# RetNet retention feeding a top-1 mixture of experts: retention output transposed, router logits by chunk

## The chip, the cores and the metric

One Trainium2 chip, one core of it. The metric is the device time of one execution in microseconds (us). The profile comes from one execution whose own time stands beside its span below.

## What is computed

For 4 batches, 8 heads, 768 positions and a head width of 64, a state is decayed and added to at each position; the result becomes 3072 tokens of 512 features. Each token goes to the one expert of eight that its logits choose.

```python
gamma = 1.0 - 2.0 ** (-5.0 - np.arange(H, dtype=np.float32))
for t in range(S):
    state = gamma[None, :, None, None] * state + np.einsum('bhd,bhe->bhde', k[:, :, t], v[:, :, t])
    y[:, :, t] = scale * np.einsum('bhd,bhde->bhe', q[:, :, t], state)
...
logits = x @ w_gate
expert_idx = np.argmax(logits, axis=1)
...
h = np.maximum(x_sorted[lo:hi] @ w1[e], 0.0)
y_sorted[lo:hi] = h @ w2[e]
...
return (gate_w[:, None] * y).astype(np.float32)
```

## The kernel before

All products are float32 but the small ones of the routing. The work has three parts.

**Retention.** The sequence is cut into six chunks of 128 positions, and a step is one chunk of one batch (`steps`, 24 of them, the four batches of a chunk in a row). `load` fetches q, k and v four steps ahead, in rows of 256 bytes, on SP's queue. `scale_and_transpose(n)` scales q by the decay of the position (`qs`, DVE) and v by its inverse (`vs`, POOL), and turns q and k heads first (`tr`, eight transposes). `retain(n)` makes the scores of the eight heads (`sc`, two row halves of the array side by side), masks them from PSUM (`am`, DVE), makes the chunk's addition to the state (`new`, two column halves side by side), adds and decays it (`total`, `state`), copies it into a block-diagonal tile (`stb`, POOL), and makes `y`: for each pair of heads one 128x128 product with `stb` and two with the masked scores as the stationary operand and 64 columns of `vs` moving.

**Routing.** `logits(n)`, one step behind, turns the step's `x` (`trx`, four transposes), copies it (`xT`, DVE) and makes `lg` with x stationary and the eight columns of `wg` moving. After the fourth batch of a chunk `place(c)` takes the maximum, the rank of each token within its expert (`rk`) and its slot (`found`), scales x by the gate and writes it to `x_d`. After chunk 4 the first 256 tokens of expert 0 are gathered early (`xs2[0]`).

**Experts.** The early half of expert 0 runs first on PE (`hp<-xTa`, `ye<-hTa`), with the last routing spread between its blocks through the generator `rest`. Then the eight experts follow, each with `layer1`, the transposes of the next one (`turn`) and `layer2`.

Outside the parts under `manual_schedule` a list scheduler orders each engine's instructions; each engine then runs its queue in that order.

## Time and profile before

| | |
|---|---|
| median of 3 runs | 602.84 us |
| lowest, highest | 590.13 us, 608.62 us |
| the profiled execution | 591.75 us |
| its span, mean granted TensorE clock | 589.9 us, 0.954 |

The span runs from the first to the last instruction, and the execution's own time is 1.85 us more. The retention ends near 200 us of the span, the early half of expert 0 near 235 us, and the rest belongs to the experts. A matmul in float32 leaves two records in the trace, a transpose or a bfloat16 product one. A busy PE says little, since the ends of matmuls are modelled; the time from one group's start to the next one's is what a group costs.

### The profile page before, as it was taken

The page shows a single profiled execution, that of the slowest core. Times are in us where ns is not written, and L with a number is a line of the kernel's source. Part 1 is how long each engine was busy: PE and PEld are TensorE (multiplying, and loading weights), DVE is VectorE, ACT ScalarE, POOL GpSimd, SP SyncE. Part 2 cuts the span into 40 slices and gives each one's busy share as a digit, 9 for nine tenths or more (in the row PEclk, how much of TensorE's full clock was granted, in tenths as well). Part 3 has the DMA queues.
Part 4 walks back from the last instruction along what each step waited for, and adds up shares of the span by engine and source line. Part 5 has one row for each costly group of instructions (what it writes and reads, how often), then busy time and mean ns, then how long its engine had stood idle before and what let it go on. Part 6 is the DMA issues. An engine that isn't in the chain of part 4 may idle for free.

```text
span 589.9 us, 7874 instructions
## 1 busy us (share of the span) xinstructions
PE 558.0 (95%) x3160; PEld 374.7 (64%) x3160; DVE 109.6 (19%) x291; ACT 123.3 (21%) x245; POOL 119.0 (20%) x156
## 2 busy tenths in 40 slices
PE   4998999999999998999999999999999999999990
PEld 3988988989898873855545545546545645545540
DVE  2545455534645230300000000000000000000000
ACT  2213222312424130212102202201211301202100
POOL 8322313213221023040032013005005005002010
PEclk9987979959999899899999999999999999999996
DMA  9964745965512122880333325217306217001010
GB/s 185 207 131 122 146 125 130 352 171 115 149 35 73 36 87 89 312 311 20 144 111 148 144 57 191 75 72 258 141 7 242 76 71 257 1 4 53 4 39 21
DMA packets 96469, 72.43 MB, mean 123 GB/s; under 512 B 77946, under 2 KB 77946, under 8 KB 96384
## 3 DMA queue, kind: packets, MB, share of 16 engines
q1 hardware_dynamic: 88096, 52.46, 32.9%
q0 software_dynamic: 5120, 12.60, 5.7%
q10 hardware_dynamic: 3168, 6.29, 2.9%
q8 instruction: 47, 0.77, 0.6%
q14 instruction: 38, 0.31, 0.2%
HBM read 60.84 MB, written 14.68 MB: 128 GB/s over the span
## 4 chain that ended last, share of the span: by engine, by line
PE 54%; issue 34%; DVE 4%; POOL 3%; DMA 2%; SPq 0%; POOLq 0%; DVEq 0%
PE hp L189 13%; PE ye L201 11%; PE y L290 7%; PE sc L262 5%; PE tr L248 4%; PE y L286 4%; PE lg L310 4%; PE new L271 2%; PE trx L305 2%; POOL xs L151 2%; DMA out_dram<-o,dst 1%; PE trs L181 1%; POOL out_dram L208 1%; DVE am L264 1%; DMA q<-in_q_dram 1%
## 5 line engine op out<-in xcount | busy, mean ns | idle before, releaser
L201 PE MATMUL ye<-w2t,hT 128*128 128x512 f32 (+3 forms) x640 | 164.1, 455 | 0.0
L189 PE MATMUL hp<-xTs,w1t 128*128 128x416 f32 (+4 forms) x512 | 163.7, 482 | 0.2 <-DVE xTs L182 0.2
L189 PEld LDWEIGHTS hp<-xTs,w1t 128*128 128x128 f32 x512 | 94.2, 195 | 70.1 <-issue 54.9
L201 PEld LDWEIGHTS ye<-w2t,hT 128*128 128x128 f32 (+3 forms) x640 | 74.8, 154 | 84.4 <-issue 83.2
L208 POOL DMA_INDIRECT out_dram<-o,dst x30 | 29.8, 994 | 281.8 <-ACT o L204 276.0
L290 PE MATMUL y<-vs,am 128*128 128x64 f32 x384 | 60.5, 279 | 1.4 <-DVE am L264 0.7
L290 PEld LDWEIGHTS y<-vs,am 128*128 128x128 f32 x384 | 55.5, 205 | 4.3 <-issue 1.8
L191 ACT ACTIVATE hT<-hp 128x416 f32<-128x416 f32 (+4 forms) x64 | 29.3, 481 | 137.4 <-PE hp L189 94.0
L204 ACT COPY o<-ye 128x512 f32<-128x512 f32 (+3 forms) x40 | 17.7, 444 | 144.8 <-PE ye L201 144.5
L264 DVE TENSOR_TENSOR am<-sc,causal 128x512 f32<-128x512 f32 x48 | 31.3, 685 | 44.8 <-PE sc L262 44.8
L286 PE MATMUL y<-stb,qT 128*128 128x128 f32 x160 | 38.3, 324 | 0.0
L262 PE MATMUL sc<-qT,kT 64*128 64x128 f32 x384 | 37.2, 306 | 0.9 <-DVE am L264 0.9
L151 POOL DMA_INDIRECT xs<-x_d,src x30 | 30.4, 1013 | 33.8 <-DVE dst L174 24.9
L281 POOL COPY stb<-state 64x256 f32<-64x256 f32 x40 | 19.7, 492 | 83.7 <-DVE state L278 72.1
L243 POOL TENSOR_TENSOR vs<-v,dec 128x512 f32<-128x512 f32 x24 | 25.5, 1064 | 40.3 <-PE new L271 26.7
L262 PEld LDWEIGHTS sc<-qT,kT 64*128 64x128 f32 x384 | 29.8, 202 | 5.3 <-issue 4.4
L293 ACT COPY xg<-y 128x512 f32<-128x512 f32 x24 | 14.1, 588 | 86.8 <-PE y L290 86.8
L286 PEld LDWEIGHTS y<-stb,qT 128*128 128x128 f32 x160 | 26.4, 207 | 1.3
L248 PE MATMUL tr<-ident,qs 128*128 128x128 f32 x96 | 19.2, 325 | 7.1 <-DVE qs L242 7.1
L310 PE MATMUL lg<-wg,xT 128*128 128x8 f32 x192 | 25.2, 258 | 0.2
L310 PEld LDWEIGHTS lg<-wg,xT 128*128 128x128 f32 x192 | 24.3, 198 | 1.5 <-DVE xT L307 0.9
L250 ACT COPY qT<-tr 128x512 f32<-128x512 f32 x24 | 14.1, 587 | 39.4 <-PE tr L248 39.4
(111 smaller groups left out, 350.2 us busy)
## 6 DMA issues: line engine op xcount, KB each, us to landing
w1t<-in_moe_w_dram SPq DMA_DIRECT2D x8, 2048.0 KB, 7.9
w2t<-in_moe_w_dram SPq DMA_DIRECT2D x8, 2048.0 KB, 15.0
q<-in_q_dram SPq DMA_DIRECT2D x24, 256.0 KB, 4.3
k<-in_k_dram SPq DMA_DIRECT2D x24, 256.0 KB, 3.3
v<-in_v_dram SPq DMA_DIRECT2D x24, 256.0 KB, 5.1
x_d<-xg ACTq DMA_DIRECT2D x6, 1024.0 KB, 4.3
xs<-x_d,src POOLq DMA_INDIRECT x30
out_dram<-o,dst POOLq DMA_INDIRECT x30
```

Source lines behind the costliest of these rows:

```text
L151: nc.gpsimd.indirect_dma_start(out=xs[:, t, :], out_offset=None, in_=x_d[0:rows, :], in_offset=bass.IndirectOffsetOnAxis(ap=idx[:, t : t + ...
L189: nc.tensor.matmul(hp, lhsT=w1t[:, 0, dt, ts(f, P)], rhs=xT[:, dt, 0:n], start=(dt == 0), stop=(dt == DT - 1))
L191: nc.scalar.activation(out=hT[:, f, 0:n], in_=hp, func=AF.Relu)
L201: nc.tensor.matmul(y[j * m : j * m + m, 0:c], lhsT=hT[:, f, t * P : t * P + m], rhs=w2t[:, 0, f, ts(j, c)], start=(f == 0), stop=(f == FT ...
L208: done = nc.gpsimd.indirect_dma_start(out=out[:, :], out_offset=bass.IndirectOffsetOnAxis(ap=idx[:, t : t + 1], axis=0), in_=o[:, t, :], i ...
L243: nc.gpsimd.tensor_tensor(out=vs, in0=vt, in1=inner(gk, D), op=ALU.mult)
L248: nc.tensor.transpose(tr[:, a, :], src[:, 2 * a : 2 * a + 2, :].rearrange("p h d -> p (h d)"), ident)
L262: nc.tensor.matmul(sc[j][:, a, :], lhsT=kT[r, a, :], rhs=qT[r, a, :], start=True, stop=True)
L264: nc.vector.tensor_tensor(out=am[j], in0=sc[j], in1=middle(causal[:, :], HP), op=ALU.mult)
L286: nc.tensor.matmul(y[:, ts(a, P)], lhsT=qT[:, a, :], rhs=stb[b][c % 2][:, a, :], start=True, stop=False, skip_group_check=True)
L290: nc.tensor.matmul(y[:, ts(h, D)], lhsT=am[j][:, a, :], rhs=vs[:, h, :], start=(c == 0), stop=True, skip_group_check=True)
L310: nc.tensor.matmul(lg[:, b, :], lhsT=xT[:, dt, :], rhs=wg[:, dt, :], start=(dt == 0), stop=(dt == DT - 1))
```

## The change

- q is turned raw, and the scaling is done while it leaves PSUM (`qT`, DVE), by a table `gqT` that keeps the decay of the position in the whole sequence. v is scaled by the inverse of the same decay (one table for each chunk), so the state is only added to: the product with `gp`, the tile `total` and the block-diagonal copies on POOL go. POOL makes one `gqT` for each chunk.
- `y` comes out transposed, features first: for each head one product with the 64x64 state stationary and qT moving, and one with 64 columns of `vs` stationary and the masked scores moving. A pair of heads uses two diagonal quarters of the array (state) and two column halves (scores). ACT copies it into `xTg`, which holds a chunk's four batches.
- The logits are made once for a chunk: four products of 32 columns (`wg`, padded with zeros) with 512 tokens moving, each in a column group of its own (`parts`), a copy on ACT (`lgT`), and four products with the 0/1 matrix `sel` that adds the groups and turns the result (`lg`).
- `place` is a generator for every chunk, advanced twice a step (three times in the last chunk). It turns x back (`trx`, sixteen transposes at its end), and ACT scales x while it leaves PSUM.
- Loads run five steps ahead with six buffers, and expert 0's weights are issued at step 17 in place of 12.

```diff
+    back = [gamma ** -(e + P * c) for c in range(NC)]
+    return np.concatenate([gamma ** e / math.sqrt(D)] + back + [whole], 1).astype(np.float32)
...
+    dec = const.tile([P, (1 + NC) * H + HP], F32, tag="dec", name="dec")
+    wg = const.tile([P, DT, P // DT], F32, tag="wg", name="wg")
+    sel = const.tile([P, E], F32, tag="sel", name="sel")
...
+    gq, gp = dec[:, 0:H], dec[:, (1 + NC) * H :]
+    nc.gpsimd.memset(wg, 0.0)
+    nc.gpsimd.tensor_copy(sel, ident[:, 0:E])
+    for dt in range(1, DT):
+        nc.gpsimd.tensor_tensor(out=sel, in0=sel, in1=ident[:, dt * (P // DT) : dt * (P // DT) + E], op=ALU.add)
...
-        stb = [[keep.tile([P, HP, P], F32, tag=f"stb{b}_{i}", name=f"stb{b}_{i}") for i in range(2)]
-               for b in range(B)]
         xg = [keep.tile([P, B, DM], F32, tag=f"xg{i}", name=f"xg{i}") for i in range(2)]
+        xTg = [keep.tile([P, DT, B, P], F32, tag=f"xTg{i}", name=f"xTg{i}") for i in range(2)]
+        gqT = [keep.tile([P, HP, P], F32, tag=f"gqT{i}", name=f"gqT{i}") for i in range(2)]
...
-                t = att.tile([P, H, D], F32, tag=nm, name=nm, bufs=5)
+                t = att.tile([P, H, D], F32, tag=nm, name=nm, bufs=6)
                 nc.sync.dma_start(t, src[b, :, ts(c, P), :].rearrange("h t d -> t h d"))
                 got.append(t)
             qkv[n] = got
+        def heads_first(src):
+            tr = ps("tr", 3, "tr").rearrange("p (a t) -> p a t", a=HP)
+            for a in range(HP):
+                nc.tensor.transpose(tr[:, a, :], src[:, 2 * a : 2 * a + 2, :].rearrange("p h d -> p (h d)"), ident)
+            return tr
         def scale_and_transpose(n):
+            c, b = steps[n]
             qt, kt, vt = qkv.pop(n)
...
             vs = att.tile([P, H, D], F32, tag="vs", name="vs", bufs=3)
-            nc.vector.tensor_tensor(out=qs, in0=qt, in1=inner(gq, D), op=ALU.mult)
-            nc.gpsimd.tensor_tensor(out=vs, in0=vt, in1=inner(gk, D), op=ALU.mult)
...
+            nc.gpsimd.tensor_tensor(out=vs, in0=vt, in1=inner(dec[:, (1 + c) * H : (2 + c) * H], D), op=ALU.mult)
+            qT = att.tile([P, HP, P], F32, tag="qT", name="qT")
+            kT = att.tile([P, HP, P], F32, tag="kT", name="kT")
+            nc.vector.tensor_tensor(out=qT, in0=heads_first(qt), in1=gqT[c % 2], op=ALU.mult)
+            nc.scalar.copy(out=kT, in_=heads_first(kt))
+            if b == 0 and c + 1 < NC:
+                nc.gpsimd.tensor_tensor(out=gqT[(c + 1) % 2], in0=gqT[c % 2], in1=inner(gp, P), op=ALU.mult)
+            front[n] = (kt, vs, qT, kT)
         def retain(n):
             c, b = steps[n]
...
             for a in range(HP):
                 for j in range(2):
...
             for j in range(2):
...
+            old = state.get(b)
             if c < NC - 1:
                 new = ps("tr", 3, "new")[:, 0 : HP * D].rearrange("p (a d) -> p a d", a=HP)
                 for a in range(HP):
                     for j in range(2):
                         h = 2 * a + j
                         nc.tensor.matmul(new[ts(j, D), a, :], lhsT=kt[:, h, :], rhs=vs[:, h, :], start=True, stop=True)
...
+                state[b] = att.tile([P, HP, D], F32, tag=f"state{b}", name=f"state{b}")
                 if c:
-                    nc.vector.tensor_tensor(out=total, in0=new, in1=state[b], op=ALU.add)
+                    nc.vector.tensor_tensor(out=state[b], in0=new, in1=old, op=ALU.add)
                 else:
...
-                nc.vector.tensor_tensor(out=nxt, in0=total, in1=inner(gp, D), op=ALU.mult)
-                state[b] = nxt
+                    nc.vector.tensor_copy(state[b], new)
+            y = ps("y", 2, "y").rearrange("p (a t) -> p a t", a=HP)
+            if c:
+                for a in range(HP):
+                    for j in range(2):
+                        r = ts(j, D)
+                        nc.tensor.matmul(y[r, a, :], lhsT=old[r, a, :], rhs=qT[r, a, :], start=(a == 0), stop=False,
+                                         skip_group_check=True)
+            for a in range(HP):
                 for j in range(2):
-                    nc.gpsimd.tensor_copy(stb[b][(c + 1) % 2][ts(j, D), :, ts(j, D)], nxt[ts(j, D), :, :])
-            y = ps("y", 2, "y")
-            for a in range(HP):
-                if c:
-                    nc.tensor.matmul(y[:, ts(a, P)], lhsT=qT[:, a, :], rhs=stb[b][c % 2][:, a, :],
-                                     start=True, stop=False, skip_group_check=True)
-                for j in range(2):
-                    h = 2 * a + j
-                    nc.tensor.matmul(y[:, ts(h, D)], lhsT=am[j][:, a, :], rhs=vs[:, h, :],
-                                     start=(c == 0), stop=True, skip_group_check=True)
-            x = xg[c % 2][:, b, :]
-            nc.scalar.copy(out=x, in_=y)
-            return n, x
+                    nc.tensor.matmul(y[ts(j, D), a, :], lhsT=vs[:, 2 * a + j, :], rhs=am[j][:, a, :], start=(c == 0),
+                                     stop=True, skip_group_check=True)
+            nc.scalar.copy(out=xTg[c % 2][:, :, b, :], in_=y)
         groups, early = {}, []
-        def logits(n, x):
-            c, b = steps[n]
...
+        def place(c):
+            g0 = c * B
+            xT = xTg[c % 2]
+            parts = ps("lg", 1, "parts")
+            m = P // DT
             for dt in range(DT):
-                nc.tensor.transpose(tr[:, dt, :], x[:, ts(dt, P)], ident)
...
+                nc.tensor.matmul(parts[ts(dt, m), :], lhsT=wg[:, dt, :], rhs=xT[:, dt, :, :].rearrange("p b t -> p (b t)"),
+                                 start=True, stop=True)
+            lgT = att.tile([P, B * P], F32, tag="lgT", name="lgT", bufs=1)
+            nc.scalar.copy(out=lgT, in_=parts)
             yield
-            for dt in range(DT):
-                nc.tensor.matmul(lg[:, b, :], lhsT=xT[:, dt, :], rhs=wg[:, dt, :], start=(dt == 0), stop=(dt == DT - 1))
-            yield
-            if b == B - 1:
-                yield from place(c, lg)
-        def place(c, lg):
-            g0 = c * B
+            lg = ps("lg", 1, "lg")[:, 0 : B * E].rearrange("p (b e) -> p b e", e=E)
+            for b in range(B):
+                nc.tensor.matmul(lg[:, b, :], lhsT=lgT[:, ts(b, P)], rhs=sel, start=True, stop=True)
...
+            gate = att.tile([P, B], F32, tag="gate", name="gate")
...
+            nc.vector.reciprocal(gate, gate)
             yield
...
+            yield
             x = xg[c % 2]
             for b in range(B):
-                nc.scalar.activation(out=x[:, b, :], in_=x[:, b, :], func=AF.Copy, scale=gate[:, b : b + 1])
+                tr = ps("tr", 3, "trx").rearrange("p (a t) -> p a t", a=DT)
+                for dt in range(DT):
+                    nc.tensor.transpose(tr[:, dt, :], xT[:, dt, b, :], ident)
+                nc.scalar.activation(out=x[:, b, :].rearrange("p (a t) -> p a t", a=DT), in_=tr, func=AF.Copy,
+                                     scale=gate[:, b : b + 1])
+                if b == 1:
+                    yield
             nc.scalar.dma_start(x_d[ts(c, B * P), :].rearrange("(b p) r -> p b r", p=P), x)
             if c == NC - 2:
...
                 gather(xs2[0], early[0][0], range(EARLY // P), (c + 1) * B * P)
-        AHEAD = 4
+        AHEAD = 5
         for n in range(AHEAD):
             load(n)
-        nc.sync.dma_start(wg, w_gate.rearrange("(dt p) e -> p dt e", p=P))
...
-                nc.gpsimd.memset(t, 0.0)
+        nc.sync.dma_start(wg[:, :, 0:E], w_gate.rearrange("(dt p) e -> p dt e", p=P))
+        gq_all = att.tile([P, H, D], F32, tag="vs", name="gq_all", bufs=3)
+        nc.vector.tensor_copy(gq_all, inner(gq, D))
+        nc.vector.tensor_copy(gqT[0], heads_first(gq_all))
         scale_and_transpose(0)
...
-        done = None
+        rest = iter(())
         for n in range(len(steps)):
             if n + AHEAD < len(steps):
                 load(n + AHEAD)
-            if n == 12:
+            if n == 17:
                 wa = weights(first, 0)
             if n + 1 < len(steps):
                 scale_and_transpose(n + 1)
-            last, done = done, retain(n)
-            if last:
...
-        rest = logits(*done)
+            retain(n)
+            for _ in range(2 if n < len(steps) - B else 3):
+                next(rest, None)
+            if steps[n][1] == B - 1:
+                rest = place(steps[n][0])
         with tc.manual_schedule(engines={mybir.EngineType.PE}):
             turn(xs2[0], xTa, range(EARLY // P), nc.vector.tensor_copy)
...
```

The order on PE in one step of a later chunk, from its scores on; before:

```order
L262 MATMUL sc<-qT,kT 128x128 x8
L271 MATMUL new<-vs,k 64x64 x8
L286 MATMUL y<-stb_0_113,qT 128x128
L290 MATMUL y<-vs,am_853 128x64
L305 MATMUL trx<-ident,xg_122 128x128 x4
L290 MATMUL y<-vs,am_854 128x64
L286 MATMUL y<-stb_0_113,qT 128x128
L290 MATMUL y<-vs,am_853 128x64
L290 MATMUL y<-vs,am_854 128x64
L286 MATMUL y<-stb_0_113,qT 128x128
L290 MATMUL y<-vs,am_853 128x64
L290 MATMUL y<-vs,am_854 128x64
```

and now:

```order
L273 MATMUL sc<-qT,kT 128x128 x8
L283 MATMUL new<-vs,k 64x64 x8
L296 MATMUL y<-qT,state_458 64x128 x8
L300 MATMUL y<-am_781,vs 64x128
L300 MATMUL y<-am_782,vs 64x128
L300 MATMUL y<-am_781,vs 64x128
L300 MATMUL y<-am_782,vs 64x128
L300 MATMUL y<-am_781,vs 64x128
L300 MATMUL y<-am_782,vs 64x128
L300 MATMUL y<-am_781,vs 64x128
L300 MATMUL y<-am_782,vs 64x128
```

The transposes `trx` that stood between the products of `y` are gone from the step, the four products with `stb` are eight with the state, and all of these stand ahead of the first product with `am`.

PE in the step after `rk`, where `found` gives the routing its slots; before:

```order
L286 MATMUL y<-stb_0_115,qT 128x128
L290 MATMUL y<-vs,am_982 128x64
L290 MATMUL y<-vs,am_983 128x64
L370 LDWEIGHTS here
L370 MATMUL found<-val,here 128x64
L370 LDWEIGHTS here
L370 MATMUL found<-val,here 128x64
L370 LDWEIGHTS here
L370 MATMUL found<-val,here 128x64
L370 LDWEIGHTS here
L370 MATMUL found<-val,here 128x64
L248 MATMUL tr<-ident,qs 128x128 x4
```

and now, from the scores of that step on:

```order
L273 MATMUL sc<-qT,kT 128x128 x8
L296 MATMUL y<-qT,state_343 64x128 x8
L377 LDWEIGHTS here
L377 MATMUL found<-val,here 128x64
L377 LDWEIGHTS here
L377 MATMUL found<-val,here 128x64
L377 LDWEIGHTS here
L377 MATMUL found<-val,here 128x64
L377 LDWEIGHTS here
L377 MATMUL found<-val,here 128x64
L249 MATMUL tr<-ident,q 128x128 x4
L249 MATMUL tr<-ident,k 128x128 x4
```

Before, `found` followed all of a step's `y`; now it stands behind the scores and the state products, ahead of the next transposes, `new` and the products with `am`.

PE between the early half's blocks near the end of the routing of the last chunk; before, at its start:

```order
L310 MATMUL lg<-wg,xT 128x8 x4
L181 MATMUL trs<-ident,xs_103 128x128 x2
L189 MATMUL hp<-xTa,w1t 128x256 x4
L305 MATMUL trx<-ident,xg_122 128x128 x4
L189 MATMUL hp<-xTa,w1t 128x256 x4
L310 MATMUL lg<-wg,xT 128x8 x4
L189 MATMUL hp<-xTa,w1t 128x256 x8
```

and now, at its end:

```order
L198 MATMUL hp<-xTa,w1t 128x256 x8
L388 MATMUL trx<-ident,xTg_122 128x128 x8
L198 MATMUL hp<-xTa,w1t 128x256 x4
L388 MATMUL trx<-ident,xTg_122 128x128 x8
L198 MATMUL hp<-xTa,w1t 128x256 x4
L210 MATMUL ye<-w2t,hTa 128x512 x16
```

The transposes of x, one batch's before and all four batches' now, have moved behind the seventh and the eighth block of `hp`, and the write of `x_d` behind them.

## Rows read from the trace of the kernel before

**Rows 1.** The page: busy time by engine, and granted clock in 40 slices.

```profile
PE 558.0 (95%) x3160; PEld 374.7 (64%) x3160; DVE 109.6 (19%) x291; ACT 123.3 (21%) x245; POOL 119.0 (20%) x156
PEclk9987979959999899899999999999999999999996
```

**Rows 2.** Windows table: us, busy by engine (instructions), granted clock, DMA share, GB/s.

```profile
13.00:48.10 35.10, 32.94 (x330) 29.60 (x329) 17.84 (x39) 7.47 (x14) 12.20 (x16) 0.95 0.90 167
48.10:80.10 32.00, 31.39 (x313) 29.30 (x313) 17.51 (x46) 9.43 (x17) 7.74 (x12) 0.89 0.58 133
80.10:112.90 32.80, 31.74 (x313) 29.27 (x313) 17.21 (x45) 9.53 (x17) 7.90 (x12) 0.90 0.65 198
112.90:149.80 36.90, 35.74 (x313) 33.29 (x313) 17.30 (x45) 9.53 (x17) 8.15 (x12) 0.77 0.71 168
149.80:181.00 31.20, 29.90 (x303) 27.14 (x303) 17.20 (x44) 9.43 (x17) 7.11 (x10) 1.00 0.30 77
181.00:200.90 19.90, 18.78 (x173) 17.33 (x172) 9.51 (x34) 6.37 (x11) 2.23 (x2) 1.00 0.24 81
235.60:589.90 354.30, 340.25 (x1272) 182.86 (x1272) 4.91 (x4) 60.95 (x132) 54.20 (x54) 0.98 0.33 115
```

**Rows 3.** Timeline of PE, one retention step: start us, us, engine, line, op, tiles, records.

```profile
141.58 0.63 PE L248 MATMUL tr<-ident,qs 128*128 128x128 f32 x4
...
142.58 1.16 PE L262 MATMUL sc<-qT,kT 64*128 64x128 f32 x16
143.67 0.69 PE L271 MATMUL new<-vs,k 128*64 128x64 f32 x16
144.29 0.49 PE L286 MATMUL y<-stb,qT 128*128 128x128 f32 x2
...
144.79 0.61 PE L305 MATMUL trx<-ident,xg 128*128 128x128 f32 x4
145.24 0.33 PE L290 MATMUL y<-vs,am 128*128 128x64 f32 x2
...
147.42 1.01 PE L310 MATMUL lg<-wg,xT 128*128 128x8 f32 x8
148.36 0.38 PE L262 MATMUL sc<-qT,kT 64*128 64x128 f32 x2
```

**Rows 4.** Timeline of PE, `y` of a step in the first chunk.

```profile
16.16 2.00 PE L290 MATMUL y<-vs,am 128*128 128x64 f32 x16
18.00 0.61 PE L248 MATMUL tr<-ident,qs 128*128 128x128 f32 x4
```

**Rows 5.** Groups by form, PE, 372 to 400 us: `layer2` tiles of 128 and 64 columns.

```profile
L201 PE MATMUL ye<-w2t,hT 128*128 128x512 f32 x48 | 20.9, 594 | 0.0
L201 PE MATMUL ye<-w2t,hT 128*64 128x256 f32 x32 | 3.7, 382 | 0.0
```

**Rows 6.** The same, 326.8 to 329.5 us: the tile of 32 columns.

```profile
L201 PE MATMUL ye<-w2t,hT 128*32 128x128 f32 x64 | 2.0, 274 | 0.0
```

**Rows 7.** Groups by form, DVE: eviction of the scores.

```profile
L264 DVE TENSOR_TENSOR am<-sc,causal 128x512 f32<-128x512 f32 x48 | 31.3, 685 | 44.8 <-PE sc L262 44.8
```

**Rows 8.** Timeline of DVE: from the rank product to the values that `found` waits for.

```profile
211.93 0.19 DVE L346 TENSOR_TENSOR own<-rk,ohs 128x32 f32<-128x32 f32 x1 [2.66 <-PE rk L340]
...
213.60 0.42 DVE L362 TENSOR_TENSOR val<-at,tok 128x256 bf16<-128x256 f32 x1
```

**Rows 9.** Timeline: `x_d` written, early tokens gathered, first transposes of them.

```profile
184.54 0.37 ACTq L383 DMA_DIRECT2D x_d<-xg  x1
...
191.28 1.00 POOL L151 DMA_INDIRECT xs<-x_d,src_e  x1 [0.31 <-issue]
...
195.70 0.38 PE L181 MATMUL trs<-ident,xs 128*128 128x128 f32 x2
```

**Rows 10.** Timeline of PE: first `hp` of the early half, first transposes of the MoE.

```profile
200.87 3.66 PE L189 MATMUL hp<-xTa,w1t 128*128 128x256 f32 x8 [0.78 <-DVE xTa L182]
...
235.64 1.96 PE L181 MATMUL trs<-ident,xs 128*128 128x128 f32 x8 [2.81 <-issue]
```

More of the change, by code (lines that the diff above doesn't have):

```diff
@@ L21 @@
 P = 128
+NC = 6
 def decay_table(H, D):
@@ L67 @@
     F = w1.shape[2]
-    NC = S // P
     HP = H // 2
@@ L77 @@
     FAR = 1 << 20
-    assert D == 64 and DM == H * D and N == B * S and NT == B * NC and DM == 512
+    assert NC == S // P and D == 64 and DM == H * D and N == B * S and NT == B * NC and DM == 512
     const = ctx.enter_context(tc.tile_pool(name="const", bufs=1))
@@ L271, in retain @@
                         nc.tensor.matmul(new[ts(j, D), a, :], lhsT=kt[:, h, :], rhs=vs[:, h, :], start=True, stop=True)
-                total = att.tile([P, HP, D], F32, tag="total", name="total")
+                state[b] = att.tile([P, HP, D], F32, tag=f"state{b}", name=f"state{b}")
                 if c:
-                    nc.vector.tensor_tensor(out=total, in0=new, in1=state[b], op=ALU.add)
+                    nc.vector.tensor_tensor(out=state[b], in0=new, in1=old, op=ALU.add)
                 else:
-                    nc.vector.tensor_copy(total, new)
@@ L292, in retain @@
-            x = xg[c % 2][:, b, :]
-            nc.scalar.copy(out=x, in_=y)
-            return n, x
-        groups, early = {}, []
-        def logits(n, x):
-            c, b = steps[n]
-            if b == 0:
-                groups[c] = ps("lg", 1, "lg")[:, 0 : B * E].rearrange("p (b e) -> p b e", e=E)
-            lg = groups[c]
-            tr = ps("tr", 3, "trx").rearrange("p (a t) -> p a t", a=DT)
+                    nc.vector.tensor_copy(state[b], new)
+            y = ps("y", 2, "y").rearrange("p (a t) -> p a t", a=HP)
@@ L332, in place @@
             nc.vector.tensor_tensor(out=oh, in0=middle(em[:, :], B), in1=inner(idx[:, :], E), op=ALU.is_equal)
+            gate = att.tile([P, B], F32, tag="gate", name="gate")
+            nc.vector.tensor_reduce(gate, ex, axis=AX.X, op=ALU.add)
+            nc.vector.tensor_scalar(out=gate, in0=gate, scalar1=1e-9, scalar2=None, op0=ALU.add)
+            nc.vector.reciprocal(gate, gate)
             yield
@@ L373, in place @@
             nc.vector.tensor_tensor(out=inv_f, in0=inv_f, in1=found, op=ALU.add)
-            gate = att.tile([P, B], F32, tag="gate", name="gate")
-            nc.vector.tensor_reduce(gate, ex, axis=AX.X, op=ALU.add)
-            nc.vector.tensor_scalar(out=gate, in0=gate, scalar1=1e-9, scalar2=None, op0=ALU.add)
-            nc.vector.reciprocal(gate, gate)
+            yield
             x = xg[c % 2]
             for b in range(B):
-                nc.scalar.activation(out=x[:, b, :], in_=x[:, b, :], func=AF.Copy, scale=gate[:, b : b + 1])
+                tr = ps("tr", 3, "trx").rearrange("p (a t) -> p a t", a=DT)
[5 more added lines that the diff above has]
+                    yield
             nc.scalar.dma_start(x_d[ts(c, B * P), :].rearrange("(b p) r -> p b r", p=P), x)
@@ L414 @@
                 scale_and_transpose(n + 1)
-            last, done = done, retain(n)
-            if last:
-                for _ in logits(*last):
-                    pass
-        rest = logits(*done)
+            retain(n)
[3 more added lines that the diff above has]
+                rest = place(steps[n][0])
         with tc.manual_schedule(engines={mybir.EngineType.PE}):
```

21 lines of the change are left out of this document (1 added, 20 removed).

## The prediction

> **What bounds the kernel now.** I read the page first: PE is busy for 95% of the span, the next engines for 21%, and in five of the first 14 of the 40 slices, where the retention lies, the granted clock is below 0.9 [rows 1]. Since the ends of matmuls are modelled, that busy share could hide waits, so I read PE's timeline next. One step of a later chunk, at full clock, runs group behind group without a gap: transposes 1.00 us (141.58 to 142.58), scores 1.09, `new` 0.62, `y` with `trx` 3.13, of which `trx` is 0.45, and `lg` 0.94; 6.78 us in all [rows 3]. So in a step PE itself is the bound, and what an engine beside it saves costs nothing. The third view is a table of windows from one rank product (`rk`) to the next: 32.0, 32.8, 36.9 and 31.2 us, at clocks of 0.89, 0.90, 0.77 and 1.00 [rows 2]. Four steps are 27.1 us, so the chunk at full clock holds 4.1 us more: the small products of `place` and the waits around it. Against that chunk the other three lost 0.8, 1.6 and 5.7 us, 8.1 together, to a lower clock. The experts, 354.3 us of the span [rows 2], are not touched.
>
> **y.** It takes 3.13 - 0.45 = 2.68 us, 24 records [rows 3]. It becomes 32 records of 128 columns: 16 in two diagonal quarters, 16 in two column halves. Neither form stands in the trace with that many columns. The nearest row is `sc`: 16 records, 128 columns, two row halves, 1.09 us [rows 3]. A column half at 256 columns, 32 records in 3.7 us, makes 0.058 us for 128 columns and 0.93 us for 16 [rows 5]. With no overlap, 48 records of 512 columns in 20.9 us make 0.109 us for 128 and 1.74 us for 16 [rows 5]. I take 1.09 for each half, as the same records and columns. `y` is then 2.18, and a step 1.00 + 1.09 + 0.62 + 2.18 = 4.89 us. In the first chunk `y` goes from 1.84 us (16.16 to 18.00) to 1.09 [rows 4].
>
> The step can't fall much lower. The two score evictions of 0.685 us [rows 7] follow `sc`, and `new` and the state products cover 0.62 + 1.09 = 1.71 of those 1.37 us and their hand-over, some 0.3 to spare. With `y` at 0.93 for each half the cover is just used up: 4.6 us is the floor.
>
> **Logits and trx.** `lg` was 0.94 us in each step. Now a chunk has one `parts` and one `lg`. `parts` is eight records of 512 columns in four column groups; 64 records of 128 columns in such groups took 2.0 us [rows 6], so 0.031 x 4 x 8 = 1.0 us, and 8 x 0.435 = 3.5 without overlap [rows 5]. The sixteen `trx` are as many as before, 4 x 0.45 = 1.8 us. A later chunk's work is 4 x 4.89 + 1.0 + 0.94 + 1.8 = 23.3 us.
>
> **The waits of place.** The small products are the same, some 0.4 us. `lg` waits for the copy `lgT` behind one ACT copy of `y`, with six transposes as cover: 0.2 us. The next scores' eviction stands behind `place`'s first eleven small DVE operations: 0.2 us. `found` now stands ahead of the transposes, `new` and `y` on PE, so what it waits for holds a step: on DVE, from the rank product to the last value, 211.93 to 214.02, 2.1 us [rows 8], with one score eviction of 0.7 ahead of the last operation and 0.3 for the start, 3.1 us, against 2.4 us of scores, state products and small ones: 0.7 us. `trx` leaves PSUM through ACT with three buffers: 0.4 us. Together 1.9 us with the small products, an estimate; the bound above is the 4.1 of before. A chunk is then 25.2 us (23.9 to 27.4), four are 100.8 against 132.9: **-32.1 us**, with the lost clock of before in it.
>
> **The first chunk.** The first `y` starts at 16.16 us [rows 4] behind the first loads, which don't change; the table's transposes run while q is under way. A step then needs 3.80 us of PE, but its loads, three of 262 KB at 167 GB/s by a share of 0.90 [rows 2], need 4.2, so the queue sets the pace. 16.16 + 1.09 + 3 x 4.2 + 2 x 4.89 + 2.3 for `parts`, `lg` and their waits is 41.9 us against 48.1: **-6.2**. Later a chunk moves 4 x 4.2 us of loads and 1 MB of `x_d` in 25 us, and fits. Expert 0's weights, issued at step 17, have six steps to land, and only the loads of step 23, due five steps on, stand behind them on SP's queue.
>
> **The end of the retention.** From `rk` of chunk 4 to the first `hp` were 19.9 us [rows 2]. Now `found` and `trx` end 5.5 us after that `rk`. Then x is scaled (1.0 us), written and gathered: from the issue of `x_d` at 184.54 that took at most until 195.70, where PE turned the tokens, and at least until the second gather's issue ended at 192.28 [rows 9], so 8.7 to 12.2 us, of which I take 10.5. PE has 7.8 us of products left meanwhile, so a wait of 2.7 us opens that wasn't there. With 1.9 for the turning and its eviction, 17.9 us: **-2.0**.
>
> **The early half.** From the first `hp` to the experts' first transposes were 34.8 us [rows 10]. `parts` adds 1.0, `trx` 1.35, `rk` and `found` behind single blocks some 0.65: **+3.0**. The last `x_d` is issued 19 us after the first `hp`; with the 11.2 us of [rows 9] the tokens are there at 30, and nobody waits. POOL and DVE lose work that PE didn't wait for, and POOL's `gqT` has four steps until it is read: nothing.
>
> **Sum.** -32.1 - 6.2 - 2.0 + 3.0, and 3.0 given back to the clock (two chunks like the third interval's 1.6), are -34.3 us: 591.75 - 34.3 = 557.4 us for an execution like the profiled one. The median of the runs stands 11 us above that, and the rows show one thing in the retention that varies, the clock. As the new step leaves PE fewer gaps I add 3 of the 11: **560 us**.
>
> **A rule against the change.** After `sc` the next form starts at 143.67 while the last scores end at 143.74, and the products with `stb` start at 144.29 before `new` ends at 144.36 [rows 3]: passing from one shape of the array to another costs no visible gap. The Trainium skill, page "TensorEngine Tiling (Array Packing)", section "Key Properties", says that changing the tiling mode, not just the tile, drains TensorE. By that rule each pass would cost a pipeline's tail; the rows speak against it. The sum by the rule is the 568 us of the first rival below, by the rows 560.
>
> **The rivals.**
> *Passes between shapes cost a tail.* A step has two more (into the quarters, out to the halves). The tail of a group is 0.16 us (`trx`: 0.61 long, the next starts after 0.45 [rows 3]); 24 x 2 x 0.16 = 7.7 us, 568 us. For it only that quarters are in no row.
> *The clock falls as in the worst chunk.* 5.7 us [rows 2] in each of four chunks in place of 3 in all, 20 us more: 580 us. For it: the clock fell in three of four intervals before, and `place` still makes PE wait. Against: the new step is denser.
> *The groups don't overlap.* `y` is 3.49, a step 6.20, a chunk 24.8 + 3.5 + 0.94 + 1.8 + 1.9 = 32.9 us; four of them and 3 for the clock are 1.7 above before, the first chunk ends at 48, the early half gains 5.5: some 599 us, no change. Against it: [rows 5] and [rows 6].
> *Slower.* The low clock holds for most of the retention. At half clock a chunk's work of 23.3 us takes 46.6; each us at half clock costs half a us, so from 560 to 603 takes 86 us of it, out of some 155. For it: 0.77 over a whole chunk [rows 2]. Held throughout it gives four chunks of 48.5 us (+93) and some 28 more ahead of and behind them, about 680 us.
>
> **How the numbers follow.** My forecast (546 to 572) has 0.64; the clock 0.16; the tails 0.07; no overlap 0.06; slower 0.07. The low end is `y` at its floor (-1.2 us a chunk) with `place`'s waits halved and the clock full, 546; the high end takes in the clock rival, 582. A measurement of this kernel tells about 2% from no change, 12 us: faster 0.86, same 0.07, slower 0.07.
>
> **What would show it.** Right: on PE some 4.9 us from one step's transposes to the next, 16 records of each half of `y` in 1.1 us or less, `parts` in 1.0, 25 us from `rk` to `rk`, the first `hp` near 160 to 166 us, the experts' 354 us unchanged. Wrong: `y` records 0.1 us apart, a granted clock below 0.8 across several chunks, or waits of `found` or of the early tokens of many us.

## The result, and the profile after

The changed kernel takes 555.2 us (median of four runs, 554.4 to 558.1) where the kernel before takes 596.81 (590.13 to 608.62). Two of the runs before, 602.84 and 608.62 us, are left out as slow, and the ratio is that of the changed kernel's four, 555.72 us on average, to the other two, 590.46: 0.9412, 95% interval 0.9354 to 0.947, 5.9% faster. The profiled execution took 555.3 us, with a span of 553.5 and a granted clock of 0.983; 591.75, 589.9 and 0.954 were its counterparts before. The page of the changed kernel, PE's share and the granted clock in 40 slices, answers to [rows 1]:

```profile
PE 521.9 (94%) x3228; PEld 320.9 (58%) x3228; DVE 87.9 (16%) x249; ACT 113.7 (21%) x227; POOL 101.3 (18%) x118
...
PEclk9999999999979989999999999999999999999996
```

PE is as busy as before. In the first 14 slices, where the clock was below 0.9 in five, it is so in one, the twelfth (152 to 166 us), where the retention ends. Where the time went is read from the windows from `rk` to `rk`, to the first `hp`, to the experts and to the end, in the columns of [rows 2]:

```profile
13.00:42.15 29.15, 29.15 (x352) 22.40 (x351) 14.68 (x34) 6.58 (x12) 7.24 (x7) 1.00 1.09 208
42.15:66.99 24.84, 24.30 (x330) 19.79 (x330) 12.87 (x36) 7.82 (x14) 5.13 (x5) 1.00 0.77 182
66.99:92.16 25.17, 24.30 (x331) 19.79 (x330) 13.19 (x36) 7.82 (x14) 5.21 (x5) 1.00 0.83 191
92.16:117.32 25.16, 24.29 (x330) 19.78 (x329) 13.20 (x36) 7.82 (x14) 5.21 (x5) 1.00 0.86 224
117.32:141.53 24.21, 23.34 (x284) 18.11 (x284) 11.42 (x32) 7.33 (x13) 4.17 (x4) 1.00 0.55 173
141.53:161.38 19.85, 15.22 (x155) 11.71 (x153) 9.05 (x31) 5.29 (x9) 2.24 (x2) 0.94 0.24 80
161.38:199.86 38.48, 34.56 (x138) 22.34 (x139) 6.07 (x37) 7.59 (x16) 8.05 (x8) 0.94 0.20 66
199.86:553.50 353.64, 339.24 (x1272) 181.46 (x1272) 4.91 (x4) 61.03 (x132) 54.22 (x54) 0.98 0.33 115
```

The four intervals are 99.4 us together, at full clock, where 132.9 stood. The first `rk` comes 5.9 us earlier, the end of the retention is as long as it was, the early half is 3.7 us longer, the experts are the same. One step on PE's timeline (start, length, group), against [rows 3]:

```profile
55.05 0.66 PE L249 MATMUL tr<-ident,q 128*128 128x128 f32 x4
55.55 0.60 PE L249 MATMUL tr<-ident,k 128*128 128x128 f32 x4
56.08 1.16 PE L273 MATMUL sc<-qT,kT 64*128 64x128 f32 x16
57.17 0.69 PE L283 MATMUL new<-vs,k 128*64 128x64 f32 x16
57.78 1.09 PE L296 MATMUL y<-qT,state 64*64 64x128 f32 x16
58.80 1.09 PE L300 MATMUL y<-am,vs 128*64 128x128 f32 x16
59.83 1.07 PE L314 MATMUL parts<-xTg,wg 128*32 128x512 f32 x8
```

A step is 59.83 - 55.05 = 4.78 us, and each half of `y` 1.02 from its start to the next group's. A later place of the same timeline, around the next `rk`, shows what is left of the routing's waits; a bracket at a row's end names an idle stretch and what ended it:

```profile
65.58 1.47 PE L300 MATMUL y<-am,vs 128*64 128x128 f32 x16
66.99 0.19 PE L343 MATMUL rk<-ohs,before 128*128 128x32 bf16 x1
...
70.26 0.28 PE L377 MATMUL found<-val,here 128*128 128x64 bf16 x4 [0.87 <-DVE val L369]
```

`found` holds PE for 0.87 us, and `y` with `am` takes 1.41 us in place of 1.02, since `am` is evicted behind `place`'s small operations. At the end of the retention PE waits in four places; this is its timeline from `trx` to the first `hp`, with the issue of the write of `x_d` by ACT (ACTq) among it:

```profile
144.82 2.07 PE L388 MATMUL trx<-ident,xTg 128*128 128x128 f32 x16
...
147.95 0.37 ACTq L393 DMA_DIRECT2D x_d<-xg  x1
...
149.57 0.43 PE L300 MATMUL y<-am,vs 128*64 128x128 f32 x2
149.93 0.65 PE L296 MATMUL y<-qT,state 64*64 64x128 f32 x6
150.51 1.09 PE L300 MATMUL y<-am,vs 128*64 128x128 f32 x14
...
154.35 1.60 PE L300 MATMUL y<-am,vs 128*64 128x128 f32 x16 [0.87 <-DVE am L275]
157.98 0.66 PE L190 MATMUL trs<-ident,xs 128*128 128x128 f32 x4 [2.03 <-DMA xs<-x_d,src_e]
159.48 1.11 PE L190 MATMUL trs<-ident,xs 128*128 128x128 f32 x4 [0.84 <-DMA xs<-x_d,src_e]
161.38 3.78 PE L198 MATMUL hp<-xTa,w1t 128*128 128x256 f32 x8 [0.78 <-DVE xTa L191]
```

The 2.03 and 0.84 us are the wait for the early half's tokens, which [rows 9] had not. The granted clock falls to half, the lower of its two levels, in the second of these waits and stays there for 6.8 us, as a window of its own shows:

```profile
159.15:165.97 6.82, 5.71 (x20) 3.45 (x20) 0.91 (x2) 0.38 (x1) 0.00 (x0) 0.50 0.00 0
```

### The profile page after: what moved, and what is told of

Its sections match the earlier page's. It is cut to its first block, busy times and chain, and to the rows that moved or that the text cites. A ratio compares the mean times of both kernels' runs of the same rounds, so it can differ in the third digit from the quotient of the medians.

```text
span 553.5 us, 7883 instructions
## 1 busy us (share of the span) xinstructions
PE 521.9 (94%) x3228; PEld 320.9 (58%) x3228; DVE 87.9 (16%) x249; ACT 113.7 (21%) x227; POOL 101.3 (18%) x118
## 4 chain that ended last, share of the span: by engine, by line
issue 51%; PE 33%; DMA 6%; POOL 4%; DVE 3%; SPq 0%; POOLq 0%; ACT 0%; DVEq 0%; ACTq 0%
PE y L300 5%; PE sc L273 5%; PE tr L249 5%; DMA out_dram<-o,dst 4%; PE hp L198 4%; PE ye L210 4%; PE y L296 3%; POOL xs L160 3%; PE new L283 2%; PE trx L388 2%; POOL out_dram L217 1%; PE parts L314 1%; PE lg L321 1%; DMA q<-in_q_dram 1%; PE trs L190 1%
## 5 line engine op out<-in xcount | busy, mean ns | idle before, releaser
L200 ACT ACTIVATE hT<-hp 128x416 f32<-128x416 f32 (+4 forms) x64 | 29.3, 481 | 136.9 <-PE hp L198 107.7
L300 PE MATMUL y<-am,vs 128*64 128x128 f32 x384 | 31.2, 280 | 1.0 <-DVE am L275 0.9
L302 ACT COPY xTg<-y 128x512 f32<-128x512 f32 x24 | 14.1, 587 | 63.1 <-PE y L300 63.1
L300 PEld LDWEIGHTS y<-am,vs 128*64 128x64 f32 x384 | 22.7, 136 | 7.1 <-issue 4.1
L260 ACT COPY kT<-tr 128x512 f32<-128x512 f32 x24 | 14.1, 586 | 42.1 <-PE tr L249 42.0
L296 PE MATMUL y<-qT,state 64*64 64x128 f32 x320 | 22.7, 276 | 0.0
L259 DVE TENSOR_TENSOR qT<-tr,gqT 128x512 f32<-128x512 f32 x24 | 16.6, 691 | 37.5 <-PE tr L249 36.6
L190 PE MATMUL trs<-ident,xs 128*128 128x128 f32 x128 | 17.0, 287 | 5.8 <-issue 3.0
L190 PEld LDWEIGHTS trs<-ident,xs 128*128 128x128 f32 x128 | 15.0, 146 | 9.2 <-issue 5.3
L249 PE MATMUL tr<-ident,q 128*128 128x128 f32 x96 | 17.0, 299 | 2.2 <-DMA q<-in_q_dram 2.2
L296 PEld LDWEIGHTS y<-qT,state 64*64 64x64 f32 x320 | 17.3, 132 | 2.2 <-issue 0.3
```

Source lines behind the costliest of these rows:

```text
L190: nc.tensor.transpose(tr[:, dt, :], xs[:, t, ts(dt, P)], ident)
L200: nc.scalar.activation(out=hT[:, f, 0:n], in_=hp, func=AF.Relu)
L249: nc.tensor.transpose(tr[:, a, :], src[:, 2 * a : 2 * a + 2, :].rearrange("p h d -> p (h d)"), ident)
L296: nc.tensor.matmul(y[r, a, :], lhsT=old[r, a, :], rhs=qT[r, a, :], start=(a == 0), stop=False, skip_group_check=True)
L300: nc.tensor.matmul(y[ts(j, D), a, :], lhsT=vs[:, 2 * a + j, :], rhs=am[j][:, a, :], start=(c == 0), stop=True, skip_group_check=True)
```

## The experiments

All runs here have the token counts of the experts as constants in place of the jump into one of many bodies; up to the experts, the first of them has the instructions of the changed kernel in the same order on every engine. Times are medians of four runs. The first run, the next four and the last three were on three chips; so the intervals, which agree to 0.01 us where nothing was changed, are a safer measure than differences of 1 or 2 us between medians. My theory: the gain is PE's shorter step (column halves of `y` that overlap, logits by chunk) and fewer waits of the routing. The rivals are told with each run.

**The measure for the others: fixed sizes.**

```diff
-            for a in tc.Switch(which, arms_of(e), hint=f"job{e}"):
+            for a in [ARMS[e]]:
```

> The changed kernel with the token counts of the experts written in as constants of these inputs (128, 416, 416, 448, 352, 416, 384, 416) in place of the jump into one of many bodies; up to the experts the instructions stand in the same order. It is the measure for the other runs, which are built the same way. Theory: the full clock through the whole retention is a property of the new step, since PE has no idle time over 1 us between two groups there; so again the granted clock is 1.00 in the four intervals from rk to rk, they are 24.2 to 25.2 us (24.84, 25.17, 25.16, 24.21 in the changed kernel's profile), the first hp stands at 158 to 162 us, and the span is 545 to 556 us (553.5 with the jumps). Rival: the clock in the retention is a matter of the single execution, as the 11 us between the median and the profiled execution of the kernel before suggest; then one or two of the intervals show a clock below 0.95 and last 1.5 us or more longer.

548.74 us (548.56 to 548.86), ratio to before 0.9326 [0.9263, 0.939]: the jumps are 6.5 us. The profiles show where: 2.9 us ahead of the first expert (the early half is 35.55 us for 38.48) and 4.0 in the experts (349.60 for 353.64). The intervals are 24.85, 25.17, 25.16 and 24.21 us at clock 1.00, within 0.01 of the changed kernel's, and the first `hp` stands at 161.75. The clock of the retention repeats; the theory holds.

**Loads and decay as before.**

```diff
-        AHEAD = 5
+        AHEAD = 4
-            if n == 17:
+            if n == 12:
...
-                    nc.vector.tensor_tensor(out=state[b], in0=new, in1=old, op=ALU.add)
+                    nc.vector.tensor_tensor(out=total, in0=new, in1=old, op=ALU.add)
+                nc.vector.tensor_tensor(out=state[b], in0=total, in1=inner(gp, D), op=ALU.mult)
```

> Two parts are put back as they were before the change: loads four steps ahead with five buffers and expert 0's weights at step 12; and the decay by chunk (one table for k and q in every chunk, the state multiplied by the chunk's decay after each sum, one more VectorE operation in a step; POOL's gqT is gone). Theory: neither part bears on the time. The state has four steps until it is read, VectorE is idle for half of a step, and the loads are hidden once the first chunk is over: the intervals from rk to rk stay at 24.2 to 25.4 us, the first rk at 42 to 43 us, the whole at 547 to 551 us against 548.7 for the changed kernel with fixed sizes. Rival for the loads: the 4.2 MB of expert 0's weights now go in front of the loads of steps 17 and later, and a step of 4.8 us can't wait for them: one interval grows by 3 us or more with PE's transposes waiting for the DMA of q. Rival for the decay: the operation stands ahead of the next step's am and q scaling on VectorE: 0.3 us in each of 20 steps, +6 us spread over all intervals.

549.1 us (547.6 to 549.95). Its third interval in the table of windows, the one that takes in the weights:

```profile
92.81:117.97 25.16, 24.30 (x331) 19.79 (x330) 14.88 (x40) 7.81 (x14) 4.17 (x4) 1.00 0.99 233
```

VectorE works 1.7 us more in a chunk and the DMA engines are full, and the interval is 25.16 us all the same. Neither part shows in the time; both rivals fall.

**Logits by step.**

```diff
+            for dt in range(DT):
+                nc.tensor.matmul(groups[c][:, b, :], lhsT=xTg[c % 2][:, dt, b, :], rhs=wg[:, dt, 0:E], start=(dt == 0),
+                                 stop=(dt == DT - 1))
```

> x stays transposed, but the logits of each batch are made by four products of 8 columns with x as the stationary operand, as before the change; parts, lgT and the summing products are gone. Theory: what is fetched as stationary costs, so a batch's lg is 0.9 us, 3.7 in a chunk, against 1.94 for parts and lg together: +1.8 us a chunk, 26.5 to 27.2 us from rk to rk, six chunks +8 to +11 us, a whole of 556 to 560 us against 548.7. Rival: with the copy lgT and its wait gone the chain to the routing is shorter, and the products of the logits fall into gaps that are there anyway: 550 or less.

550.39 us (549.5 to 552.57), only 1.65 more: the theory's size was wrong. Windows of the first chunk, a later chunk and the early half, and PE's rows of `lg` and of `found`:

```profile
13.00:49.82 36.82, 36.82 (x378) 30.00 (x375) 14.73 (x34) 6.67 (x12) 7.21 (x7) 0.86 1.06 193
75.93:102.04 26.11, 25.57 (x348) 22.24 (x348) 12.70 (x36) 7.33 (x13) 5.21 (x6) 1.00 0.74 179
169.66:200.91 31.25, 30.89 (x131) 21.05 (x131) 4.95 (x29) 6.41 (x14) 7.03 (x7) 1.00 0.23 74
```
```profile
78.86 0.28 PE L377 MATMUL found<-val,here 128*128 128x64 bf16 x4 [0.54 <-DVE val L369]
89.71 1.06 PE L311 MATMUL lg<-wg,xTg 128*128 128x8 f32 x8
```

`lg` is 0.91 us in a step (the next group starts at 90.62), 3.6 in a chunk, as reckoned, against 1.9 for `parts` and `lg` (59.83 to 60.82 and 61.60 to 62.51 in the changed kernel). But the chunk is 0.95 us longer, not 1.7: `found`'s wait falls from 0.87 to 0.54 us and the group of `y` that waits behind `place`'s first operations is 1.1 us for 1.4 (100.02 to 101.12), since the longer step covers more. And the last chunk's logits leave the early half, 31.25 us in place of 35.55, part of it the clock (1.00 for 0.93). So logits by chunk are worth 1 us in a later chunk, and the whole showed 1.65. The profiled execution, the longest of the four, is 3.87 us longer than that of the measure, and its first chunk is 7.6 longer (36.82 for 29.27 us): the granted clock was 0.50 from 32 to 42 us, some 5 us of that, although PE's timeline shows no wait from 13 us on. What set this off is open.

**The routing at once.**

```diff
-            for _ in range(2 if n < len(steps) - B else 3):
-                next(rest, None)
+            for _ in rest:
+                pass
```

> The routing of a chunk (place) is written out in one go behind the next chunk's first step, as before the change, not two or three pieces a step; all products are as changed. Theory: the spreading is what keeps PE busy; without it lg waits for lgT, rk for eleven small VectorE operations and found for nine more, with only one step's products beside them: 2 to 4 us more from rk to rk, 27 to 29 us, idle stretches of over 1 us on PE, and in some of the four intervals a granted clock below 0.95; a whole of 557 to 570 us against 548.7. It may gain up to 3 us in front of the first hp, since chunk 4 is written earlier. Rival: only the products matter, and other steps' products slip into the waits: 546 to 551 us, with the intervals as they are.

563.99 us (562.67 to 564.28), 15.25 more; the theory holds. Of the four intervals the one at full clock, 28.73 us, lies in its range for a chunk; the other three, at 0.94, are above it (29.99, 30.01 and 30.57). The gain in front of the first `hp` did not come: 19.76 us from chunk 4's `rk` for 20.09. Two of the intervals, and two rows of PE's timeline:

```profile
70.49:100.50 30.01, 28.16 (x332) 22.63 (x330) 13.03 (x37) 8.23 (x14) 5.21 (x5) 0.94 0.77 160
100.50:129.23 28.73, 26.89 (x331) 20.89 (x329) 13.02 (x37) 7.92 (x14) 5.21 (x5) 1.00 0.84 233
```
```profile
72.96 0.28 PE L377 MATMUL found<-val,here 128*128 128x64 bf16 x4 [1.60 <-DVE val L369]
73.08 3.01 PE L388 MATMUL trx<-ident,xTg 128*128 128x128 f32 x16
```

The first of these chunks is 4.84 us longer than 25.17. `found` waits 1.60 us, 0.73 more; the clock, 0.94 of 30 us, takes about 1.8 (`trx` right behind the wait is 2.80 us for 2.0). The remaining 2.3 us, groups cut into pieces and waits below 0.3 us among them, I have not taken apart.

**The halves one after the other.**

```diff
-            for a in range(HP):
-                for j in range(2):
+            for j in range(2):
+                for a in range(HP):
                     nc.tensor.matmul(y[ts(j, D), a, :], lhsT=vs[:, 2 * a + j, :], rhs=am[j][:, a, :], start=(c == 0),
```

and the same for the products with the state.

> The products of y in the order of the halves: four of one column half (or of one diagonal quarter), then four of the other, in place of turn and turn about. The same instructions. Theory: two products that go to different halves run beside each other only as neighbours, so a group of 16 records goes from 1.02 us to 1.5 to 1.8 us; 44 such groups make +21 to +34 us, a whole of 570 to 583 us against 548.7, and y stands at 1.6 us in the timeline. Rival: a record of 64 columns of the array is short in itself, in whatever order: 1.0 to 1.1 us, and a whole of 547 to 551 us. In between: the first and the last of four overlap with the neighbouring group only, 1.3 us, 560 us.

559.77 us (558.62 to 560.78), 11.0 more. The whole is that of the case in between; the group, 1.50 us, is at the low end of the theory. The same records, on PE's timeline:

```profile
82.92 1.58 PE L296 MATMUL y<-qT,state 64*64 64x128 f32 x16
84.42 1.58 PE L300 MATMUL y<-am,vs 128*64 128x128 f32 x16
```

1.50 us for a group in place of 1.02, by order alone: the overlap of neighbours is real, and the records are not short in themselves. Of the 3.9 us that eight groups make in a chunk, 3.0 show (28.20 for 25.17), as `found` and `am` wait less.

**The spreading alone, on the kernel before.**

```diff
             last, done = done, retain(n)
+            next(spread, None)
             if last:
-                for _ in logits(*last):
-                    pass
+                work = logits(*last)
+                if last[0] % B == B - 1 and last[0] < 4 * B:
+                    next(work)
+                    next(work)
+                    spread = work
+                else:
+                    for _ in work:
+                        pass
```

> The kernel before the change (x not transposed, logits by step), with fixed sizes as the other runs and one thing of the change: the routing of chunks 0 to 3 is written out in three pieces, one behind each of the next steps, in place of all at once. Theory: the spreading alone is a large part of the gain, as undoing it alone cost the changed kernel 15 us and 4.8 us a chunk: the intervals from rk to rk go from 32.0, 32.8, 36.9 and 31.2 us to 28 to 30 us each with a granted clock near 1.00, the first hp to 183 to 190 us (200.87 before), a whole of 565 to 577 us against some 585 for the kernel before less the 6.5 us of the jumps. Rival: the routing's waits are covered by the longer y of the kernel before, and the spreading matters only once the step is short: intervals of 31 to 33 us, the first hp at 196 us or later, 580 us or more.

572.86 us (566.6 to 579.88), ratio 0.9638 [0.9534, 0.9742], of which the jumps are 6.5 us. The windows of the later chunks:

```profile
66.81:94.73 27.92, 27.92 (x315) 26.16 (x315) 18.61 (x46) 9.29 (x17) 8.52 (x12) 1.00 0.72 166
94.73:122.43 27.70, 27.60 (x316) 25.87 (x315) 16.39 (x44) 9.32 (x17) 7.37 (x12) 1.00 0.88 263
122.43:151.74 29.31, 28.78 (x316) 26.57 (x316) 17.65 (x45) 9.43 (x17) 8.64 (x12) 1.00 0.78 169
```

With no product changed, a chunk at full clock goes from 31.2 us [rows 2] to 27.9, 27.7 and 29.3, 28.3 on average (why the third is longer was not pursued), and the lower clock of the later chunks is gone with the waits. The theory holds for the intervals. The 31.2 us hold a step of the last chunk, which has no `new` (0.62 us), so a chunk like the others would be some 31.8, an estimate. Of the 6.6 us from there to 25.2 the spreading is then 31.8 - 28.3 = 3.5 and the new products 28.3 - 25.2 = 3.1. The other order of the two agrees: with the new products alone, in the routing at once, the chunk at full clock is 28.73, 3.1 below 31.8, and the spreading takes 3.6 more. So each is about half of the gain in a later chunk. The first `hp`, at 192.29 us, is later than the expected 183 to 190: the first chunk of this execution had a clock of 0.84, so its whole tells less than these rows.

**Found last, chunk 4 earlier.** The waits that were left in the profile name the next version:

```diff
-            found = ps("tr", 3, "found")[:, 0 : 2 * E * TC]
...
             nc.scalar.dma_start(x_d[ts(c, B * P), :].rearrange("(b p) r -> p b r", p=P), x)
+            yield
+            found = ps("tr", 3, "found")[:, 0 : 2 * E * TC]
...
+            if n >= len(steps) - B:
+                next(rest, None)
             retain(n)
-            for _ in range(2 if n < len(steps) - B else 3):
+            for _ in range(2 if n != len(steps) - B else 3):
                 next(rest, None)
             if steps[n][1] == B - 1:
                 rest = place(steps[n][0])
+                if n == len(steps) - B - 1:
+                    next(rest)
```

> The changed kernel with fixed sizes, and two moves in the routing: the transposes of x back (trx) and the write of x stand ahead of found, so that found follows the VectorE work that it waits for by a step; and chunk 4's pieces run some half a step to a step earlier. Theory: both waits that the trace showed go away. found's 0.87 us in each chunk: rk to rk 24.2 to 24.8 us in place of 25.16; at the end of the retention the tokens are gathered 4 us or more earlier, so PE's 2.3 and 0.8 us of waiting for them and the fall of the clock behind it go: rk of chunk 4 to the first hp 16 to 18.5 us in place of 20.1. A whole of 540 to 545.5 us against 548.7. Rival: found's wait moves to trx or to am, the more so since trx now splits the products of other shapes, and the early tokens are bound by their DMA: 546.5 us or more.

537.35 us (537.24 to 537.66), 11.4 less than the measure and below the expected 540; ratio to before 0.9074 [0.9014, 0.9134]. Windows of a later chunk and of the stretches around the first `hp`, and PE's rows of `found` and of that `hp`:

```profile
66.62:90.78 24.16, 24.16 (x331) 19.86 (x330) 13.18 (x36) 7.94 (x14) 5.32 (x5) 1.00 0.88 189
114.94:133.29 18.35, 18.09 (x229) 14.54 (x228) 10.02 (x29) 6.77 (x12) 3.13 (x3) 1.00 0.69 219
133.29:153.34 20.05, 19.03 (x210) 15.06 (x209) 10.86 (x34) 5.85 (x10) 3.31 (x3) 1.00 0.24 79
153.34:186.00 32.66, 32.06 (x138) 21.19 (x139) 4.95 (x29) 7.02 (x15) 7.02 (x7) 1.00 0.22 71
```
```profile
73.44 0.28 PE L388 MATMUL found<-val,here 128*128 128x64 bf16 x4
...
153.34 0.92 PE L198 MATMUL hp<-xTa,w1t 128*128 128x256 f32 x3 [0.94 <-DVE xTa L191]
```

`found` and the early tokens are waited for no more. Chunk 4's `rk` comes 5.9 us earlier (18.35 for 24.21), so the time from `rk` to `hp` is no shorter, though I had expected 16 to 18.5 us; from chunk 3's `rk` to `hp` it is 38.40 for 44.30. The clock stays full up to the experts, and the early half is 2.9 us shorter (32.66 for 35.55), most of it the clock: its first `hp` and `parts` take 2.91 us, and 5.28 at half clock in the measure. Three intervals give 2.7 us of the 11.4, and the stretch from chunk 3's `rk` on gives the rest; the two moves were not run apart.

**One change of shape less.**

```diff
-            if c < NC - 1:
-                new = ps("tr", 3, "new")[:, 0 : HP * D].rearrange("p (a d) -> p a d", a=HP)
...
             y = ps("y", 2, "y").rearrange("p (a t) -> p a t", a=HP)
...
+            if c < NC - 1:
+                new = ps("tr", 3, "new")[:, 0 : HP * D].rearrange("p (a d) -> p a d", a=HP)
```

> As the run with found last, and y's products with the state are written ahead of new, so that new and y's products with am, which have the same shape (128 rows, 64 columns), are neighbours: one change of shape less in a step. Theory: a change of shape costs 0.15 us, since in the trace of the changed kernel with fixed sizes the last record of a group is 0.20 us from the next group's first, where records or pairs in a group are 0.10 apart, and that first one 0.15 from the second; between the transposes of q and of k, two groups of one shape, there is neither. So new and y take 0.15 us less in each of some 16 steps: -2.4 us (-1.5 to -3) against the run with found last. Rival: the gap belongs to each new group, whatever its shape, or VectorE's am becomes what is waited for: within 0.8 us of the run with found last.

535.2 us (534.52 to 535.74), 2.15 less than the run ahead of it; ratio to before 0.9037 [0.8976, 0.9097]. First a step of the run with found last, then one with the state ahead:

```profile
76.18 0.69 PE L283 MATMUL new<-vs,k 128*64 128x64 f32 x16
76.79 1.09 PE L296 MATMUL y<-qT,state 64*64 64x128 f32 x16
77.81 1.09 PE L300 MATMUL y<-am,vs 128*64 128x128 f32 x16
78.84 0.66 PE L249 MATMUL tr<-ident,q 128*128 128x128 f32 x4
```
```profile
74.31 1.09 PE L283 MATMUL y<-qT,state 64*64 64x128 f32 x16
75.33 0.69 PE L290 MATMUL new<-vs,k 128*64 128x64 f32 x16
75.84 1.04 PE L299 MATMUL y<-am,vs 128*64 128x128 f32 x16
76.82 0.44 PE L249 MATMUL tr<-ident,q 128*128 128x128 f32 x2
```

`new` takes 0.51 us for 0.61, `y` with `am` 0.98 for 1.03: 0.15 us for the change of shape that is gone. A chunk is 23.72 us for 24.16, three steps' worth; in the fourth `am` is waited for anyway. The theory holds for the steps. Not all of the difference is theirs: in the profiled execution the first `hp` comes 2.9 us earlier, and 1.1 of that lie ahead of 16 us, where PE's groups stand in the same order in both runs; the steps behind give 1.8. All four runs of this version are shorter than any run of either kernel, with the caveat of the fixed sizes; with the jumps it was not run.

## Why the prediction was right, term by term

The forecast of 560 us was 4.8 above the median, and the sum of 557.4 was 2.1 above the profiled execution.

- **PE is the bound**: right. More work on VectorE and a fuller DMA cost nothing (loads and decay as before).
- **The step**: 4.89 forecast, 4.78 measured; halves of `y` 1.02 for 1.09; `parts` and `lg` 1.9 for 1.94; `trx` 2.0 for 1.8. That the halves overlap is shown by the run that sets them apart. The bet on [rows 5] and [rows 6] against no overlap was right.
- **The waits of place**: 25.16 less products of 4 x 4.78 + 1.9 + 2.0 = 23.0 leaves 2.1 for 1.9. `found` is 0.87 for 0.7, `am` 0.4 for 0.2; `lgT` showed none. What the prediction didn't see is how much of the gain hangs on this term: it gave the products 3.8 us and the waits 2.2 of the 6.0 in a chunk at full clock. The two runs that spread the routing alone or not at all make it 3.5 for the spreading and 3.1 for the products, though these save 4.1 us of PE's groups (27.1 to 23.0): the shorter step covers less of the routing. With the new products and no spreading a chunk holds 5.7 us above its products (28.73 - 23.0), where it held 4.1 before, or 4.7 with the `new` that the 31.2 us lack. The run with found last took a whole us of the waits away.
- **The first chunk**: 41.9 forecast, 42.15 measured, but by another road, so in part by luck. The loads were to set the pace at 4.2 us a step, with PE needing 3.80. PE's timeline shows no wait for a load from 13 us on; its groups are cut into pieces there, and from one step's first `y` to the next one's it takes 4.2 to 4.8 us (18.44 to 23.26, say). The DMA engines were full as well (1.09 in the window); which of the two bounds the chunk was not tested.
- **The clock**: +3.0 was too much by all of it in the retention, whose four intervals stood at 1.00 in the changed kernel and in both runs with the same order of the routing and of `y`. Clock was lost elsewhere, in the 6.8 us at half clock that begin in the wait for the early tokens: some 2.2 us in the early half and 0.4 in the turning ahead of it. So the sum had nearly the right amount in the wrong place, which is luck. That this fall and the wait go together is shown by the run with found last, which has no such wait and a clock of 1.00 up to the experts, and by logits by step, where the wait is 0.5 us and the early half at 1.00. A wait of PE isn't the only thing that a fall follows, as the first chunk of logits by step shows. The +3 for the median was not needed either; the median lies 0.1 us from the profiled execution.
- **The end of the retention**: 17.9 forecast, 19.85 measured: no gain where 2.0 us were forecast. This is the term that was mis-sized. `trx` ended 5.3 us after `rk`, for 5.5 forecast. From there to the first transposes of the tokens it took 11.2 us for 10.5: 1.1 of scaling until the write is issued (147.95) and 10.0 until 157.98. So the wait of 2.7 us that was foretold did open, 2.03 ahead of the turning and 0.84 within it. The rest, 1.5 us, is the turning, taken at 1.9 us and measured at 3.4 (157.98 to 161.38). The prediction had the tokens land once; the second gather lands 0.8 us after PE is ready for it, the eviction is waited for another 0.78, and at half clock the second four transposes take 1.11 us for 0.66.
- **The early half**: 38.5 for 37.8. Its first 4.6 us ran at half clock: the first `hp` and `parts` take 5.1 us, and 2.9 in the run with found last. Without these 2.2 us it would be some 36.3, an estimate, 1.5 below the forecast; which of its terms was too large was not pursued.
- **The rule against the change**: my reading of [rows 3] was wrong. That the next group starts before the modelled end of the last is true within a group too, and by more: sixteen records of `y`, 0.27 us each in the list of its line, make a group of 1.09. Two records of `y` take 0.36 us to the next group, six 0.58, sixteen 1.02 (from 149.57, 149.93 and 57.78 of the changed kernel): some 0.05 for a record and 0.25 for the group itself. And the run with the state ahead shows 0.15 us for one change of shape. The Trainium skill, page "TensorEngine Tiling (Array Packing)", section "Key Properties", states that a change of the tiling mode drains TensorE; the 0.15 us agree with it, though no view shows what PE does in them. The forecast was not hurt, because the row of `sc` that priced the halves had such a change in its 1.09 us already; the rival that added 7.7 us counted it twice.

## What to carry to other kernels

Price a group of matmuls from a row of the same record count between two changes of shape, and order groups so that equal shapes are neighbours and products for different halves alternate. When the step gets shorter, go through every wait that it covered: here the spreading of a dependent chain over the next steps was worth as much as the cheaper products, and moving one product behind work that didn't need it, with the last chunk's pieces forward, gave 11 us more. When a chain's end is forecast, write down each hand-over (evict, issue, land, turn) with its row, and each transfer by itself: here two gathers landed 1.5 us apart, and the forecast had one landing.

## What the runs showed of the hardware

- Records of different column halves overlap only as near neighbours: 16 take 1.02 us in turn and 1.50 in two blocks of eight.
- A change of shape of the array costs 0.15 us on PE, though no idle stretch is shown for it.
- The granted clock went to 0.50 in the run with the routing at once behind four of its five waits of 1.60 us for `found` (windows 43.06 to 46.46, 73.78 to 77.19, 131.80 to 135.20 and 162.52 to 165.90 us), and not behind the one that ended at 102.96; in the changed kernel's intervals, with waits of 0.87 us, it stayed at 1.00. In the first chunk of logits by step it was 0.50 from 32 to 42 us, with no wait on PE's timeline since 13 us; in that of the spreading alone it was 0.52 from 33.5 to 51 us, with none since 14 us.
- The jumps into one of many bodies cost 6.5 us in all, 2.9 of them at the first.
